# Two single-query attention blocks on one core: loads of 2 MB in place of 1 MB, scores by one product and one reduction, and a new order of the start

## The chip, the cores and the metric

The kernel runs on one core of a Trainium2 chip. The metric is the device time of one execution in microseconds. Of the kernel before there are six timed runs: median 1459.83 us, lowest 1456.88, highest 1462.38.

## What is computed

Two decoder blocks, A and B, each take one token x of 512 values and a cache of keys and values in bf16. Cut to what matters:

```
q      = x @ wq                                  # 32 heads of 128
scores = q . k_cache * 128 ** -0.5               # per head, over all cached rows
p      = softmax(scores)
o      = p @ v_cache
out    = o (all heads) @ wo                      # 512 values
A: 32 heads, each with its own cache of 32768 rows
B: 32 heads over 8 caches (4 heads share one), only the last 4096 rows of 32768
result = concatenate(A, B)
```

A's caches are 32 x 32768 rows x 256 bytes, twice: 537 MB. B reads 17 MB, and wq and wo of both blocks are 4 MB each. So each byte of a cache is read once and used for one (A) or four (B) multiplications.

## The kernel before, in words

A unit is one cache: 8 units of B (4096 rows, four queries) and 32 of A (32768 rows, one query), in that order. A unit is worked in chunks of 4096 rows: 1 for B, 8 for A, 264 chunks in all. A chunk of K or V is one DMA of 1 MB in which each of the 128 partitions takes 32 consecutive rows of the cache, 8 KB in one piece. All loads are issued by SP, in program order.

Step s of the main loop (L530) does k_phase for chunk s and v_phase for chunk s - 10 (V_LAG). So V is read ten chunks behind K, when the softmax of its unit is done. K chunks have 6 buffers (tiles kn), V chunks 5 (tiles vn).

The scores of an A chunk (k_phase, L401) are split by SPLITS over three engines, by tiles of 128 rows:

- 8 tiles on PE: transpose K (L380, tile ktp in PSUM), copy it to SBUF (L262, tile kts), multiply with the query (L384, tile qk).
- 17 tiles on VectorE, one instruction each: L450 multiplies a tile with qb, the query copied to all partitions, and sums it up, into Ssb. Its full product (junkd) is thrown away.
- 7 tiles: one VectorE product in f32 (L431, tile prod), and 7 sums on ScalarE (L440, junka).

A B chunk does all its 32 tiles on PE. After the last chunk of a unit come the maximum on VectorE (L300, mpart), a maximum over partitions on GpSimd (L274, mrow), a broadcast through PE (L266, bc), and the exponential on ScalarE (L283, P). For A this waits until the VectorE work of the next chunk is written out (LAG_MAX). VectorE's instructions are held in program order by dependencies that the function dve adds.

PV of A (v_phase, L498) multiplies four tiles at a time, 128x512, into PSUM (tile o); the last unit uses single tiles (L508, tile oT). finalize divides by the sum and multiplies with wo (L334), which is loaded in groups of eight heads, 1 MB in rows of 1 KB (L321).

The start (L521 to L526): three K chunks of B, then the whole query projection of B and of A. Each loads wq in four groups of 1 MB with rows of 2 KB (L194), and A's also builds qb, head by head, through a diagonal matrix on VectorE (L219) and a product on PE (L220).

A tile's buffer is handed on when the last instruction that reads it is done, and SP waits in order: a load that waits for its buffer holds back all loads behind it.

Of the kernel before, what the change touches and what calls it, by code (L numbers as in the profile page):

```python
# [17 lines left out]
CHUNK_ROWS = 4096  # L18
TG = 8
V_LAG = 10  # L20
K_BUFS = 6
V_BUFS = 5
KT_BUFS = 4
PROD_BUFS = 3
# [3 lines left out]
SPLITS = ((8, 17, 7),)  # L28
# [5 lines left out]
N_PRE = 3  # L34
FIN_DEFER = 1
CHAIN_DVE = 1
RECIP_DEFER = 4
TAIL_KPOOL = 1
WO_B_STEP = 6
QA_STEP = -1  # L40

# [29 lines left out]
def kernel(  # L71
# [54 lines left out]
    wpool = ctx.enter_context(tc.tile_pool(name="w", bufs=4))  # L126
# [23 lines left out]
    def make_model(name, x, wq, wo, hq, d_model, dout, out_off, want_qb):  # L150
# [17 lines left out]
        m.out_ps = None  # L168
        m.qb = cpool.tile([P, hq, DH], BF16, name=f"qb_{name}") if want_qb else None
# [3 lines left out]
    mA = make_model("A", A_x, A_wq, A_wo, HQA, D_A, DOUT_A, 0, use_vec)  # L173
    mB = make_model("B", B_x, B_wq, B_wo, HQB, D_B, DOUT_B, DOUT_A, False)

    def q_projection(m):
# [11 lines left out]
        xT_sb = cpool.tile([P, m.KC], BF16, name=f"xT_{m.name}")  # L188
        nc.vector.tensor_copy(xT_sb[:], xT_ps[:])
        Q_ps = ps_m.tile([P, m.HQ], F32, tag="misc", name=f"Q_ps_{m.name}")  # L190
        hpg = m.hpg
        for grp in range(m.n_groups):
            wq_sb = wpool.tile([P, m.KC, hpg * DH], BF16, tag="w", name=f"wq_{m.name}_{grp}")
            nc.sync.dma_start(  # L194
                out=wq_sb[:],
                in_=m.wq[:, grp * hpg * DH : (grp + 1) * hpg * DH].rearrange("(kc p) c -> p kc c", p=P),
            )
            for hl in range(hpg):
                h = grp * hpg + hl
                for kc in range(m.KC):  # L200
                    nc.tensor.matmul(
                        Q_ps[:, h : h + 1],
                        lhsT=wq_sb[:, kc, hl * DH : (hl + 1) * DH],
                        rhs=xT_sb[:, kc : kc + 1],
                        start=(kc == 0),
                        stop=(kc == m.KC - 1),
                    )
        nc.vector.tensor_copy(m.qT[:], Q_ps[:])
        if m.qb is not None:
            qT32 = cpool.tile([P, m.HQ], F32, name=f"qT32_{m.name}")  # L210
            nc.vector.tensor_copy(qT32[:], m.qT[:])
            HB = 4
            for h0 in range(0, m.HQ, HB):
                nh = min(HB, m.HQ - h0)
                qb_ps = ps_m.tile([P, HB, DH], F32, tag="misc", name=f"qb_ps_{m.name}_{h0}")
                for hl in range(nh):
                    h = h0 + hl
                    dg = junkpool.tile([P, P], BF16, tag="diag", name=f"diag_{m.name}_{h}")
                    nc.vector.tensor_scalar_mul(dg[:], ident[:], qT32[:, h : h + 1])  # L219
                    nc.tensor.matmul(qb_ps[:, hl, :], lhsT=ones_bf[:], rhs=dg[:], start=True, stop=True)  # L220
                nc.vector.tensor_copy(m.qb[:, h0 : h0 + nh, :], qb_ps[:, 0:nh, :])

    units = []
    for g in range(HKVB):
        units.append(
            _Unit(
                mB,
                len(units),
                B_k_cache[0, g, SKB - WIN : SKB, :],
                B_v_cache[0, g, SKB - WIN : SKB, :],  # L230
                REP,
                mB.qT[:, g * REP : (g + 1) * REP],
                mB.oT[:, g * REP : (g + 1) * REP],
                g * REP,
            )
        )
    for h in range(HA):
        units.append(
            _Unit(
                mA,  # L240
                len(units),
# [351 lines left out]
```

## Time and profile before

| | |
|---|---|
| median of six runs | 1459.83 us |
| the profiled execution | 1456.88 us |
| its span, first to last instruction | 1455.1 us |
| bytes read from HBM | 570.43 MB, 392 GB/s over the span |
| VectorE busy | 1242.7 us (85%) |
| PE busy | 1018.1 us (70%) |
| ScalarE busy | 878.2 us (60%) |
| median from issue to landing, K of A | 20.8 us |

How to read the views. The page gives for each engine the busy time, its share of the span and the count of instructions. A line of a DMA queue has packets, MB, and the time that the packets took as a share of 16 engines' time; q1 carries the program's loads, q8 and q14 carry instructions to the engines. A line of packets counts those under 512 B (mostly the completion signals of loads), under 2 KB and under 8 KB, each including the smaller ones. A line of windows has the stretch in us, its length, the busy time and the count of instructions of PE, PEld (weight loads), DVE (VectorE), ACT (ScalarE) and POOL (GpSimd), the granted PE clock, the DMA share and GB/s. A line of groups has source line, engine, operation, output and inputs, count, then busy time in us and mean ns of one, then the idle time before them and who ended it. A line of the order of time has start, duration, engine and line; SPq is SP's issue of a DMA.

### The profile page before, as it was taken

To read this page: it belongs to the slowest core of one execution; us is meant where nothing else is said; L and a number is where in the kernel's file an instruction comes from. 1 tells how busy PE (TensorE), PEld (TensorE's weight loads), DVE (VectorE), ACT (ScalarE), POOL (GpSimd) and SP (SyncE) were. 2 spreads that over 40 slices of the span, in tenths; PEclk is the share of its full clock that TensorE was granted. 3 is DMA by queue.
4 is the path that set the end of the run, shared out by engine and by line. 5 is a ranking of instruction groups with operands and counts; after the bars stand their busy time and mean duration, and the time that the engine had idled before them with its cause. 6 is when DMAs were issued, how large, how long until landed. Compare 5 with 4: busy or idle time off the path is not lost.

```text
span 1455.1 us, 31071 instructions
## 1 busy us (share of the span) xinstructions
PE 1018.1 (70%) x7872; PEld 506.1 (35%) x7872; DVE 1242.7 (85%) x9110; ACT 878.2 (60%) x4412; POOL 77.2 (5%) x128
## 2 busy tenths in 40 slices
PE   5684777677766677777676777767677676767775
PEld 5552333333333333333333333333333333333333
DVE  2588999989998998999999899999988899998982
ACT  1274777666566666576566565666666656666652
POOL 0113000000000000000000000000000000000000
PEclk7555988878788878798688786888877778888877
DMA  9699999999998999999998999999999899999995
GB/s 373 250 396 370 383 419 420 420 421 419 415 411 320 423 419 420 410 421 420 399 377 339 402 420 421 419 420 406 407 377 398 325 420 420 421 420 396 418 387 215
DMA packets 88762, 572.44 MB, mean 393 GB/s; under 512 B 8707, under 2 KB 16901, under 8 KB 20998
## 3 DMA queue, kind: packets, MB, share of 16 engines
q1 hardware_dynamic: 88582, 570.46, 95.9%
q8 instruction: 61, 1.00, 0.3%
q14 instruction: 119, 0.97, 0.2%
HBM read 570.43 MB, written 0.00 MB: 392 GB/s over the span
## 4 chain that ended last, share of the span: by engine, by line
issue 55%; DMA 20%; PE 14%; ACT 5%; POOL 4%; DVE 2%; SPq 1%; ACTq 0%; POOLq 0%; DVEq 0%
DMA kn<-in_A_k_cache_dram 10%; DMA vn<-in_A_v_cache_dram 9%; PE o L498 7%; ACT kts L262 3%; POOL mrow L274 3%; PE ktp L380 2%; ACT P L283 1%; DMA wq_B<-in_B_wq_dram 1%; PE bc_negb L266 1%; PE qk L384 1%; POOL srow L292 1%; PE oT L357 1%; DVE junkd L450 1%; PE S L384 0%; POOL nrow L276 0%
## 5 line engine op out<-in xcount | busy, mean ns | idle before, releaser
L450 DVE SCALAR_TENSOR_TENSOR junkd<-kn,qb_A 128x128 f32<-128x128 bf16 x4352 | 942.8, 284 | 0.0
L498 PE MATMUL o<-vn,P 128*4 128x512 bf16 x1984 | 605.6, 460 | 17.3 <-DMA vn<-in_A_v_cache_dram 17.1
L440 ACT ACTIVATE junka<-prod 128x128 bf16<-128x128 f32 x1792 | 527.4, 299 | 3.6 <-DVE prod L431 3.6
L262 ACT COPY kts<-ktp 128x1024 bf16<-128x1024 bf16 x266 | 268.8, 1010 | 328.4 <-PE ktp L380 310.6
L431 DVE TENSOR_TENSOR prod<-kn,qb_A 128x896 f32<-128x896 bf16 x256 | 278.7, 1089 | 131.8 <-DMA kn<-in_A_k_cache_dram 110.3
L450 DVE DVE_READ_ACCUMULATOR junkd<-kn,qb_A 128x1 f32 x4352 | 346.5, 80 | 0.0
L440 ACT ACTIVATION_READ_ACCUMULATOR junka<-prod 128x1 f32 x1792 | 340.3, 190 | 0.0
L384 PE MATMUL qk<-qT_A,kts 128*128 128x1 bf16 x2048 | 91.8, 166 | 284.0 <-ACT kts L262 283.6
L498 PEld LDWEIGHTS <-P 128*4 128x4 bf16 x1984 | 172.5, 95 | 301.4 <-issue 167.7
L380 PE MATMUL ktp<-ident,kn 128*128 128x128 bf16 x2304 | 212.8, 247 | 20.2 <-DMA kn<-in_A_k_cache_dram 14.0
L380 PEld LDWEIGHTS <-kn 128*128 128x128 bf16 x2304 | 157.1, 110 | 124.1 <-issue 77.8
L384 PEld LDWEIGHTS <-kts 128*128 128x128 bf16 x2304 | 79.9, 100 | 337.4 <-ACT kts L262 334.7
L274 POOL CROSS_LANE_REDUCE mrow<-mpart 128x1 f32<-128x1 f32 (+1 forms) x40 | 46.8, 1169 | 1260.8 <-DVE mpart L300 1256.2
L279 ACT COPY negb<-bc_negb 128x1 f32<-128x1 f32 (+1 forms) x40 | 6.4, 160 | 117.5 <-PE bc_negb L266 117.5
L357 PE MATMUL oT<-ident,o 4*128 4x1 f32 x248 | 43.1, 290 | 20.6 <-ACT o L354 20.6
L357 PEld LDWEIGHTS oT<-ident,o 4*128 4x128 f32 x248 | 40.4, 243 | 43.5 <-ACT o L354 43.5
L266 PE MATMUL bc_negb<-nrow,ones_row 1*128 1x1 f32 (+1 forms) x80 | 18.1, 294 | 48.0 <-POOL nrow L276 46.5
L367 ACT ACTIVATE oT_A<-oT,rinv 128x1 bf16<-128x1 f32 x32 | 8.4, 263 | 61.3 <-PE oT L357 45.8
L354 ACT COPY o<-o 4x512 f32<-4x512 f32 x31 | 17.8, 575 | 37.4 <-PE o L498 37.4
L266 PEld LDWEIGHTS bc_negb<-nrow,ones_row 1*128 1x128 f32 x80 | 14.8, 230 | 69.5 <-POOL nrow L276 66.2
L463 ACT COPY Ssb<-qk 128x8 f32<-128x8 f32 x256 | 37.3, 146 | 0.5 <-PE qk L384 0.5
L260 DVE COPY kts<-ktp 128x1024 bf16<-128x1024 bf16 x22 | 15.0, 687 | 22.1 <-PE ktp L380 19.2
(49 smaller groups left out, 252.8 us busy)
## 6 DMA issues: line engine op xcount, KB each, us to landing
kn<-in_A_k_cache_dram SPq DMA_DIRECT2D x256, 1024.0 KB, 20.8
vn<-in_A_v_cache_dram SPq DMA_DIRECT2D x256, 1024.0 KB, 20.6
kn<-in_B_k_cache_dram SPq DMA_DIRECT2D x8, 1024.0 KB, 12.9
vn<-in_B_v_cache_dram SPq DMA_DIRECT2D x8, 1024.0 KB, 11.2
wq_B<-in_B_wq_dram SPq DMA_DIRECT2D x4, 1024.0 KB, 13.8
wq_A<-in_A_wq_dram SPq DMA_DIRECT2D x4, 1024.0 KB, 10.4
wo_B<-in_B_wo_dram SPq DMA_DIRECT2D x4, 1024.0 KB, 16.5
wo_A<-in_A_wo_dram SPq DMA_DIRECT2D x4, 1024.0 KB, 21.7
```

Of the source, the lines that this page charges most:

```text
L262: nc.scalar.copy(dst, src)
L266: nc.tensor.matmul(bc_ps[:, 0:n], lhsT=ones_row[0:1, :], rhs=row[0:1, 0:n], start=True, stop=True)
L274: nc.gpsimd.tensor_reduce(out=mrow[:], in_=mpart[:], axis=AX.C, op=ALU.max)
L354: nc.scalar.copy(o4_sb[:], u.oT_ps[:, :])
L357: nc.tensor.matmul(src[:, 0:1], lhsT=o4_sb[0:PVG, jl * DH : (jl + 1) * DH], rhs=ident32[0:PVG, jl : jl + 1], start=(jl == 0), stop=(jl == ...
L380: nc.tensor.transpose(KTp[:, j8, :], KN[:, j0 + jj * tg + j8, :], ident[:])
L384: nc.tensor.matmul(dst_fn(jj * tg + j8), lhsT=KTs[:, j8, :], rhs=u.q_ap, start=True, stop=True)
L431: nc.vector.tensor_tensor(out=prod[:], in0=KN[:, jz : jz + nza, :], in1=qb.rearrange("p (o d) -> p o d", o=1).to_broadcast([P, nza, DH]), ...
L440: nc.scalar.activation(out=junk_a[:], in_=prod[:, jl, :], func=ACT.Copy, accum_out=S[:, t0 + jz + jl, :],)
L450: nc.vector.scalar_tensor_tensor(out=junk_d[:], in0=KN[:, j, :], scalar=1.0, in1=qb, op0=ALU.mult, op1=ALU.mult, accum_out=S[:, t0 + j, :],)
L463: nc.scalar.copy(S[:, t0 : t0 + npe, :], qk_ps[:, :, :])
L498: nc.tensor.matmul(u.oT_ps[:, :], lhsT=u.P_sb[:, t0 : t0 + PVG, :].rearrange("p t n -> p (t n)"), rhs=VN[:, jg * PVG : (jg + 1) * PVG, :]. ...
```

## The change

Sizes. A chunk of A has 8192 rows, so an A unit has 4 chunks, a DMA moves 2 MB, and each partition takes 16 KB in one piece. B's units stay one chunk of 4096 rows. K has 4 buffers and V 3, of 2 MB each. The split of an A chunk is 16, 34 and 14 tiles, twice that of before. V runs 5 chunks behind K.

Scores on VectorE. The 34 tiles are done by one product with bf16 output (L528, tile prodv, one buffer) and one reduction along the rows (L536). prod is bf16 as well (L510).

Order. After each of the first eight A units stands one B unit (INTERLEAVE). At the start the first group of A's query projection comes first, then two K chunks. The other seven groups of A and B are done one per step (q_group, L210 and L217). W buffers for wq and wo are 3 instead of 4. B's heads, which now finish between A's, are projected with wo in groups of eight into an SBUF tile (parts) and added up by VectorE; A keeps its sum in PSUM.

The diff, cut to its core:

```diff
-CHUNK_ROWS = 4096
+CHUNK_ROWS = 8192
-V_LAG = 10
-K_BUFS = 6
-V_BUFS = 5
+V_LAG = 5
+K_BUFS = 4
+V_BUFS = 3
-PROD_BUFS = 3
+PROD_BUFS = 2
+W_BUFS = 3
-SPLITS = ((8, 17, 7),)
+SPLITS = ((16, 34, 14),)
-N_PRE = 3
+N_PRE = 2
-RECIP_DEFER = 4
+RECIP_DEFER = 2
+INTERLEAVE = 1
+A_FIRST = 1
+Q_STAGED = 1
+Q_EARLY_STEPS = 1
...
-            prod = prodpool.tile([P, nza, DH], F32, tag="prod", name=f"prod_{u.idx}_{g}")
+            prod = prodpool.tile([P, nza, DH], BF16, tag="prod", name=f"prod_{u.idx}_{g}")
...
-        for jl in range(ndve):
-            j = npe + jl
-            junk_d = junkpool.tile([P, DH], F32, tag="junk_d", name=f"junkd_{u.idx}_{g}_{jl}")
+        if ndve:
+            pv = prodpool.tile([P, ndve, DH], BF16, tag="prodv", bufs=1, name=f"prodv_{u.idx}_{g}")
             dve(
-                nc.vector.scalar_tensor_tensor(
-                    out=junk_d[:],
-                    in0=KN[:, j, :],
-                    scalar=1.0,
-                    in1=qb,
-                    op0=ALU.mult,
-                    op1=ALU.mult,
-                    accum_out=S[:, t0 + j, :],
+                nc.vector.tensor_tensor(
+                    out=pv[:],
+                    in0=KN[:, npe : npe + ndve, :],
+                    in1=qb.rearrange("p (o d) -> p o d", o=1).to_broadcast([P, ndve, DH]),
+                    op=ALU.mult,
+                )
+            )
+            dve(
+                nc.vector.tensor_reduce(
+                    out=S[:, t0 + npe : t0 + npe + ndve, :].rearrange("p t n -> p (t n)"),
+                    in_=pv[:], axis=AX.X, op=ALU.add,
                 )
             )
...
+        q_setup(units[0].model)
+        q_setup(mB if units[0].model is mA else mA)
+        q_group(q_stage.pop(0)[0])
+        for s in range(min(N_PRE, n_steps, K_BUFS - 1)):
+            u0, g0 = chunks[s]
+            pre_kn[(u0.idx, g0)] = k_load(u0, g0)
...
+                if q_stage and s >= Q_EARLY_STEPS - 1:
+                    mm, _grp = q_stage.pop(0)
+                    q_group(mm)
```

More of the change, by code (lines that the diff above doesn't have):

```diff
@@ new lines @@
+    units = []
+    if INTERLEAVE:
+        gb = 0
+        for h in range(HA):
+            units.append(make_a_unit(h, len(units)))
+            if gb < HKVB:
+                units.append(make_b_unit(gb, len(units)))
+                gb += 1
+        while gb < HKVB:
+            units.append(make_b_unit(gb, len(units)))
+            gb += 1
+    else:
+        for g in range(HKVB):
+            units.append(make_b_unit(g, len(units)))
+        for h in range(HA):
+            units.append(make_a_unit(h, len(units)))
@@ L405, in k_phase @@
             KN = k_load(u, g)
-        vec_ok = N == 1 and u.model.qb is not None and J % TG == 0
+        split = SPLITS[a_chunk_cnt[0] % len(SPLITS)]
+        vec_ok = (
+            N == 1
+            and u.model.qb is not None
+            and sum(split) == J
+            and split[0] % u.tg == 0
+        )
         if not vec_ok:
```

214 lines of the change are left out of this document (140 added, 74 removed).

## The prediction

> **What bounds the kernel now.** I read the page's totals first, then the DMA queues, then short windows of the start, the end and one slow place in the middle, then the groups of VectorE. The totals name two busy resources, the DMA engines and VectorE:
>
> ```profile
> span 1455.1 us, 31071 instructions
> PE 1018.1 (70%) x7872; PEld 506.1 (35%) x7872; DVE 1242.7 (85%) x9110; ACT 878.2 (60%) x4412; POOL 77.2 (5%) x128
> q1 hardware_dynamic: 88582, 570.46, 95.9%
> q8 instruction: 61, 1.00, 0.3%
> ```
>
> The loads keep 16 DMA engines 95.9% busy. VectorE has 1243 us of work in 1455, less than the transfers take. In the undisturbed middle the engines are full, at about 420 GB/s:
>
> ```profile
> 500.00:525.00 25.00, 20.31 (x94) 8.95 (x94) 22.12 (x165) 12.19 (x63) 0.99 (x3) 0.52 1.01 419
> ```
>
> So a load that only comes earlier gains nothing there. The end shows more. The DMA view of the last 12 us, one window of them (PE, PEld, VectorE, ScalarE and GpSimd busy, clock, DMA share, GB/s), and the order of time behind it:
>
> ```profile
> DMA packets 52, 0.38 MB, mean 31 GB/s; under 512 B 7, under 2 KB 7, under 8 KB 7
> q1 hardware_dynamic: 51, 0.36, 7.2%
> q8 instruction: 1, 0.02, 0.5%
> 1440.00:1442.00 2.00, 1.01 (x32) 0.93 (x32) 0.00 (x0) 0.00 (x0) 0.00 (x0) 0.50 0.06 25
> 1450.30 1.01 PE L508 MATMUL oT<-P,vn 128*128 128x1 bf16 x32 [1.46 <-DMA vn<-in_A_v_cache_dram]
> 1452.95 0.26 SPq L562 DMA_DIRECT2D out_dram<-res_sb  x1
> ```
>
> From 1437.5 to 1449.5 the loads fill 7.2% of 16 engines, which is one engine (1/16 is 6.25%). It carries 44 rows of 8 KB alone while 15 engines have finished, and the last V chunk waits for it. The one instruction fetch of these 12 us is there too: 0.5% of 16 x 12 us is 0.96 us. In the middle the same engine shows itself after the reload of wo (1 KB rows), where SP sits in one issue for 12 us and the traffic falls to a sixteenth:
>
> ```profile
> 450.37 12.35 SPq L392 DMA_DIRECT2D kn<-in_A_k_cache_dram  x1
> 458.00:460.00 2.00, 0.56 (x5) 0.55 (x6) 2.00 (x12) 0.11 (x1) 1.30 (x2) 0.91 0.06 25
> ```
>
> I read this as one engine that lags 8 to 13 us behind the others, because every load gives each engine the same sixteenth and this one fetches PE's code as well (in the last 12 us only PE has instructions left). If so, the kernel's time is that engine's work. I sum it, with durations from two windows, one with 8 KB rows only (475 to 700 us) and one with the 2 KB rows of wq (12 to 31 us), and the window in which the traffic sets in:
>
> ```profile
> DMA packets 12902, 94.07 MB, mean 418 GB/s; under 512 B 1429, under 2 KB 1429, under 8 KB 1429
> q1 hardware_dynamic: 12874, 93.76, 100.8%
> DMA packets 3677, 7.33 MB, mean 386 GB/s; under 512 B 113, under 2 KB 114, under 8 KB 3675
> q1 hardware_dynamic: 3675, 7.29, 103.8%
> 2.00:4.00 2.00, 0.00 (x0) 0.00 (x0) 0.00 (x0) 0.02 (x1) 0.00 (x0) 1.00 0.74 295
> ```
>
> An 8 KB row takes 0.314 us (44 rows in 7.2% of 192 us; 0.317 in the middle window, 3629 us over 11,445 rows). A 2 KB row takes 315.6 us / 3562 = 0.0886 us. For a 1 KB row I take 0.055, between half of that and the whole. One engine then has 528 K and V loads x 8 rows x 0.314 = 1326 us, 8 wq loads x 32 rows x 0.0886 = 23, 8 wo loads x 64 x 0.055 = 28, and 61 fetches x 0.96 = 59: 1436 us. Its time goes from about 2 us to 1450, 1448 us. The difference of 12 is idle time, and I find most of it at the start:
>
> ```profile
> 50.00:52.00 2.00, 0.92 (x5) 0.41 (x4) 1.24 (x4) 0.00 (x0) 0.00 (x0) 0.50 0.10 41
> 54.00:56.00 2.00, 0.96 (x32) 0.87 (x31) 1.01 (x3) 1.18 (x8) 1.22 (x3) 0.50 0.00 0
> 58.00:60.00 2.00, 1.86 (x29) 1.33 (x27) 0.69 (x1) 1.10 (x3) 0.68 (x1) 0.50 0.00 0
> 64.00:66.00 2.00, 2.00 (x34) 2.00 (x32) 0.95 (x2) 0.68 (x5) 0.68 (x1) 0.50 0.30 41
> ```
>
> Nothing moves from 51 to 60 us, and little around 64: the B units come first, their K loads fill the six buffers, and SP waits for PE and the softmaxes.
>
> **The change part by part.**
>
> **Rows of 16 KB.** 256 K and 256 V loads of A become 128 and 128, with half the rows, each 16 KB. Bytes are the same. What can go is the fixed part of a row. From 2 KB to 8 KB a row grows by 0.314 - 0.0886 = 0.225 us for 6 KB, so 8 KB more cost 0.300 and a 16 KB row 0.614, against 0.628 for two of 8 KB. The bounds are 0.601 (no fixed part at all) and 0.628 (a row goes out as two packets of 8 KB). I take 0.614, on the line of the two measured sizes. One engine carries 16,384 x 2 / 16 = 2048 such rows: 2048 x 0.0135 = **28 us less** (0 to 55).
>
> **PE's fetches.** PE's order has 15,041 rows before and after. The 61 fetches stay, **0 us**. VectorE's order falls from 4760 rows to 542, but its fetches are not seen in the tail on the late engine.
>
> **The start.** The order of SP's loads before, where the idle time lies (kn are K chunks, vn V chunks), and after from the first row:
>
> ```order
> L321 DMA wo_B_1221<-in_B_wo_dram 128x8x512
> L392 DMA kn_0_1229<-in_B_k_cache_dram 128x4096
> L392 DMA kn_0_1332<-in_A_k_cache_dram 128x4096
> L392 DMA kn_1_1412<-in_A_k_cache_dram 128x4096
> L392 DMA kn_2_1491<-in_A_k_cache_dram 128x4096
> L486 DMA vn_0_1564<-in_B_v_cache_dram 128x4096
> ```
>
> ```order
> L466 DMA kn_0_213<-in_A_k_cache_dram 128x8192
> L466 DMA kn_1_215<-in_A_k_cache_dram 128x8192
> L210 DMA wq_B_217<-in_B_wq_dram 128x4x1024
> L210 DMA wq_B_327<-in_B_wq_dram 128x4x1024
> L210 DMA wq_B_436<-in_B_wq_dram 128x4x1024
> L466 DMA kn_2_472<-in_A_k_cache_dram 128x8192
> L210 DMA wq_B_547<-in_B_wq_dram 128x4x1024
> L466 DMA kn_3_583<-in_A_k_cache_dram 128x8192
> L210 DMA wq_A_658<-in_A_wq_dram 128x4x1024
> L466 DMA kn_0_723<-in_B_k_cache_dram 128x4096
> ```
>
> Before, the first V stood behind eight B chunks and three A chunks; now one wq group is followed by 2 MB chunks with wq loads between them. I followed this by hand at 420 GB/s. The first chunk lands near 12 us, VectorE takes 8.3 us each (below), K buffers come free at 20, 29, 38 and 46 us, while the loads issued by then last until 45, 50, 60 and 65. So nothing starves, with one narrow place: PE waits for A's first softmax, behind it in PE's order stands the use of wq_A's third group, and SP's wo_B load waits for that buffer. That softmax holds a slow step:
>
> ```profile
> 124.90 13.94 POOL L274 CROSS_LANE_REDUCE mrow<-mpart 128x1 f32<-128x1 f32 x1 [37.34 <-DVE mpart L300]
> ```
>
> If it takes 14 us again, PE is free at 63 to 64 us, just when the queue runs dry. I keep 4 of the 12 idle us: **8 us less** (0 to 12).
>
> **VectorE.** One chunk before and after (junkd is a 128-element product with its sum, prod and prodv are products of several tiles, Ssb the scores):
>
> ```order
> L450 SCALAR_TENSOR_TENSOR junkd_4_15_2698,Ssb_2204<-kn_4_2630,qb_A 128x128
> L450 SCALAR_TENSOR_TENSOR junkd_4_16_2700,Ssb_2204<-kn_4_2630,qb_A 128x128
> L310 RECIPROCAL rrow_2713<-srow_2288 1x1
> L431 TENSOR_TENSOR prod_5_2741<-kn_5_2719,qb_A 128x896
> L450 SCALAR_TENSOR_TENSOR junkd_5_0_2757,Ssb_2204<-kn_5_2719,qb_A 128x128
> ```
>
> ```order
> L536 TENSOR_REDUCE Ssb_1514<-prodv_0_1584 128x34
> L510 TENSOR_TENSOR prod_1_1652<-kn_1_1611,qb_A 128x1792
> L528 TENSOR_TENSOR prodv_1_1682<-kn_1_1611,qb_A 128x4352
> L536 TENSOR_REDUCE Ssb_1514<-prodv_1_1682 128x34
> L345 RECIPROCAL rrow_1704<-srow_1447 1x1
> ```
>
> The 34 small products of 8192 rows become one product of 4352 elements and one reduction. Their prices from these groups:
>
> ```profile
> L431 DVE TENSOR_TENSOR prod<-kn,qb_A 128x896 f32<-128x896 bf16 x256 | 278.7, 1089 | 131.8 <-DMA kn<-in_A_k_cache_dram 110.3 <-ACT junka L440 10.6 <-ACT Ssb L463 8.5
> L260 DVE COPY kts<-ktp 128x1024 bf16<-128x1024 bf16 x22 | 15.0, 687 | 22.1 <-PE ktp L380 19.2 <-ACT kts L262 2.6
> L300 DVE TENSOR_REDUCE mpart<-Ssb 128x1 f32<-128x256 f32 x32 | 13.2, 412 | 1.4 <-ACT Ssb L463 1.2
> L221 DVE CAST qb_A<-qb_ps_A 128x512 bf16<-128x512 f32 x8 | 5.5, 686 | 0.4 <-PE qb_ps_A L220 0.4
> ```
>
> From 256 to 896 elements the price grows by (1089 - 412) / 640 = 1.058 ns each. The reduction of 4352 is 1.089 + 3456 x 0.001058 = 4.75 us. The products now write bf16, and with 16-bit data on every side a copy of 1024 elements costs what one of 512 costs with f32 in it (687 against 686 ns). So I take the products at half rate: 1.09 us for 1792 elements and, as for 2176, 2.44 for 4352. A chunk is 8.3 us, or 2.04 + 4.75 + 4.75 = 11.5 if they stay at full price. The one engine needs (1455 - 28 - 8) / 128 = 11.1 us per chunk of K and V. So VectorE is hidden, **0 us**, and stays hidden until a chunk passes about 10.7 (other VectorE work, 49 us over 128 chunks, takes 0.4). [...]
>
> **Fewer buffers.** The PV products of before:
>
> ```profile
> L498 PE MATMUL o<-vn,P 128*4 128x512 bf16 x1984 | 605.6, 460 | 17.3 <-DMA vn<-in_A_v_cache_dram 17.1
> ```
>
> 4 K and 3 V buffers of 2 MB hold 14 MB, against 11 MB before. A K buffer comes back 8.3 us after landing and is wanted again four chunks on, 44 us later. V's PV needs about 16 matmuls x 460 ns = 7 us of 33. Hidden; cost 0.
>
> **The tail.** The last V chunk has 64 matmuls instead of 32 behind its landing, 1.01 us more: **+1**.
>
> Sum: 1455.1 - 28 - 8 + 1 = 1420 us span. The profiled execution took 1456.88 us, 1.8 more than its span, and the median of the runs is 1459.83, 3.0 above that execution. So 1420 + 1.8 + 3.0 = **1425 us**. A measurement here can tell about 0.2%, 3 us, from no change.
>
> **The rivals.**
>
> *Rows go out as 8 KB packets.* Then 28 us stay: 1453. For it: no row of this trace carries K or V in a larger packet. Against: 8 KB rows stayed whole, and nothing shows a limit there. It is the upper end.
>
> *No single engine is the bound.* Then the mean engine counts: its 95.9 + 0.3% of 1455.1 is 1400 us, less 28, with 2 ahead, 5 behind and 4 idle: 1383 + 4.8, so 1388. The tail row of one engine alone speaks against it. [...]
>
> *VectorE becomes the bound* (slower). If the broadcast operand qb keeps the products at full price, a chunk is 11.5 us, above the 10.7 where it decides: 12 to the first chunk + 128 x 11.5 + 49 + 17 for the last softmax, 256 matmuls and the end = 1550, with 4.8, 1555. For it: no TENSOR_TENSOR of the trace runs at half rate, since all write f32. Against: the two copies above.
>
> *The narrow place at the start, or a softmax that comes late at unit boundaries.* PE would hold K buffers; some 15 us come back: 1440.
>
> **How the numbers follow.** Forecast 0.62; 8 KB packets 0.18; start or boundaries 0.08; no single engine 0.06; VectorE 0.06. The range goes from 1408 (a 16 KB row of about 0.606, halfway to its lower bound) to 1454 (the 8 KB case); it leaves out the rivals at 1388 and 1555 and the far ends of the row price, about 0.17. Within 3 us of 1460 falls only the edge of the 8 KB case, 0.03. Faster 0.91, slower 0.06.
>
> **What would show it.** Right: about 34,800 packets of K and V (128 x 256 + 128 x 16) instead of 528 x 128 = 67,584, steady windows near 428 GB/s, no empty windows before 70 us, q8 still at 61 packets, one engine alone at the end, TENSOR_TENSOR of 4352 near 2.4 us, VectorE near 1110 us. Wrong: packets of 8 KB still, q8's engine not last, VectorE above 95%, or K loads that wait for VectorE in the middle.

## The result, and the profile after

The changed kernel takes 1373.85 us (median of 8 runs, 1373.45 to 1374.2) against 1459.42 us of the kernel before in the same jobs (16 runs). The ratio is 0.9412, 95% interval [0.9403, 0.9421]. The forecast was 1425 us with a range from 1408 to 1454: the direction was right, the size was not. 86 us went, 35 were forecast.

The page of the changed kernel, totals and DMA queues:

```profile
span 1372.3 us, 21605 instructions
PE 976.9 (71%) x7872; PEld 501.3 (37%) x7872; DVE 1079.6 (79%) x541; ACT 869.6 (63%) x4293; POOL 101.5 (7%) x128
DMA packets 51824, 571.82 MB, mean 417 GB/s; under 512 B 4611, under 2 KB 12805, under 8 KB 16902
q1 hardware_dynamic: 51718, 570.45, 98.7%
q8 instruction: 61, 1.00, 0.3%
q14 instruction: 45, 0.37, 0.1%
```

The engines are fuller (98.7% against 95.9%), and 51,824 - 16,902 = 34,922 packets have 8 KB or more: the rows of 16 KB went out whole (128 x 256 of them, 128 x 16 rows of 8 KB and the 61 + 45 packets of q8 and q14 make the same 34,922). TensorE's fetches (q8, which rises to 94 where number 3 adds instructions of TensorE) stayed at 61. The row that the prediction did not use is the last one. Before, it read:

```profile
q14 instruction: 119, 0.97, 0.2%
```

q14 brings instructions in pieces of 8 KB (0.97 MB in 119 packets). 74 of 119 pieces are gone, and VectorE's instructions fell from 9,110 to 541. The prediction named VectorE's order in rows and left it at that.

Windows of the changed kernel at its start and at its end (length, busy time and count of PE, PEld, VectorE, ScalarE and GpSimd, clock, DMA share, GB/s):

```profile
0.00:25.00 25.00, 10.17 (x176) 8.32 (x176) 16.79 (x24) 12.93 (x60) 1.09 (x8) 1.00 0.93 363
50.00:75.00 25.00, 16.87 (x171) 10.49 (x171) 19.11 (x38) 10.78 (x47) 2.37 (x6) 0.95 1.03 404
1347.00:1352.00 5.00, 4.40 (x21) 1.61 (x19) 0.15 (x1) 1.32 (x4) 0.55 (x2) 1.00 1.00 426
1352.00:1357.00 5.00, 3.56 (x80) 3.15 (x81) 0.00 (x0) 0.44 (x3) 0.00 (x0) 0.88 0.51 213
1357.00:1362.00 5.00, 2.01 (x74) 1.93 (x73) 0.00 (x0) 0.00 (x0) 0.00 (x0) 0.50 0.06 26
1362.00:1367.00 5.00, 1.99 (x75) 1.91 (x73) 0.00 (x0) 0.00 (x0) 0.00 (x0) 0.50 0.06 23
```

The empty stretch at 50 to 75 us is gone (189 GB/s there before, row in number 8). The end still shows one DMA engine working alone (0.06 is one sixteenth), now for about 10 us. So the form of the bound stayed, one engine alone at the end, and that end comes 86 us earlier.

VectorE's groups after (busy us, mean ns of one, idle time before them):

```profile
L536 DVE TENSOR_REDUCE Ssb<-prodv 128x34 f32<-128x4352 bf16 x128 | 599.8, 4686 | 4.3
L528 DVE TENSOR_TENSOR prodv<-kn,qb_A 128x4352 bf16<-128x4352 bf16 x128 | 309.4, 2418 | 0.0
L510 DVE TENSOR_TENSOR prod<-kn,qb_A 128x1792 bf16<-128x1792 bf16 x128 | 139.7, 1091 | 206.8 <-DMA kn<-in_A_k_cache_dram 170.3 <-ACT junka L519 29.2 <-ACT kts L297 3.3
```

4.69, 2.42 and 1.09 us, within 2% of what was worked out beforehand. VectorE waits for K 170 us in all. The other way round it is less: SP's K loads (line 466) wait for VectorE 23 times, 89 us in all, and the DMA share of 98.7% says that the transfers hardly notice.

Now the two places where the prediction had found the late engine alone, closer: windows of 3 us of the kernel before, in 40 slices of 75 ns. A slice shows GB/s where a packet starts (109 for 8 KB, 218 for 16 KB). The first is in the middle, behind the reload of wo:

```profile
GB/s 0 109 0 0 0 109 0 0 0 0 109 0 0 0 109 0 0 0 109 218 0 0 0 0 0 0 0 0 0 0 0 109 0 0 0 109 0 0 0 109
q1 hardware_dynamic: 8, 0.06, 6.0%
q8 instruction: 1, 0.02, 2.2%
q14 instruction: 1, 0.01, 0.7%
```

The second is in the tail:

```profile
GB/s 0 0 0 109 0 0 0 0 109 0 0 0 109 0 218 0 109 0 0 0 109 0 0 0 109 0 0 0 109 0 0 0 109 0 0 0 0 109 0 0
q1 hardware_dynamic: 10, 0.07, 5.9%
q8 instruction: 1, 0.02, 2.0%
```

The lone engine starts a row every four to five slices, 0.31 us. In the tail the 16 KB fetch of q8 falls between two beats and the beat goes on: the fetch is on another engine. In the middle, the piece of q14 (the packets put it at the fourth 109) takes a beat for itself, and the row behind it takes 13 slices, 0.97 us, in place of four. In the trace's packets the piece takes 0.33 us and the row 0.66 us more than its neighbours, 0.99 us together. That is where 1 us per fetch could come from, on the engine that ends last. A fetch of q8 (the 218) runs beside this row, so this window alone does not say which of the two fetches slowed it; the tail, where the rows beside the q8 fetch keep their 0.31 us, speaks for q14.

### The profile page after: what moved, and what is told of

The parts are those of the page before. It is cut to its first block, busy times and chain, and to the rows that moved or that the text cites. A ratio compares the mean times of both kernels' runs of the same rounds, so it can differ in the third digit from the quotient of the medians.

```text
span 1372.3 us, 21605 instructions
## 1 busy us (share of the span) xinstructions
PE 976.9 (71%) x7872; PEld 501.3 (37%) x7872; DVE 1079.6 (79%) x541; ACT 869.6 (63%) x4293; POOL 101.5 (7%) x128
## 2 busy tenths in 40 slices
DMA packets 51824, 571.82 MB, mean 417 GB/s; under 512 B 4611, under 2 KB 12805, under 8 KB 16902
## 3 DMA queue, kind: packets, MB, share of 16 engines
q1 hardware_dynamic: 51718, 570.45, 98.7%
## 4 chain that ended last, share of the span: by engine, by line
issue 78%; POOL 6%; PE 5%; DMA 4%; ACT 3%; DVE 3%; SPq 0%; ACTq 0%; POOLq 0%; DVEq 0%
POOL srow L327 5%; PE o L579 2%; DMA kn<-in_A_k_cache_dram 2%; DMA vn<-in_A_v_cache_dram 2%; PE bc_negb L301 2%; ACT P L318 2%; POOL mrow L309 1%; DVE Ssb L536 1%; ACT kts L297 1%; POOL nrow L311 1%; DVE prodv L528 1%; PE ktp L454 0%; ACT negb L314 0%; ACT junka L519 0%; DVE prod L510 0%
## 5 line engine op out<-in xcount | busy, mean ns | idle before, releaser
L536 DVE TENSOR_REDUCE Ssb<-prodv 128x34 f32<-128x4352 bf16 x128 | 599.8, 4686 | 4.3
L519 ACT ACTIVATE junka<-prod 128x128 bf16<-128x128 bf16 x1792 | 525.7, 302 | 10.9 <-DVE prod L510 10.9
L519 ACT ACTIVATION_READ_ACCUMULATOR junka<-prod 128x1 f32 x1792 | 347.7, 194 | 0.0
L579 PEld LDWEIGHTS <-P 128*4 128x4 bf16 x1984 | 187.6, 98 | 409.3 <-issue 274.2
L528 DVE TENSOR_TENSOR prodv<-kn,qb_A 128x4352 bf16<-128x4352 bf16 x128 | 309.4, 2418 | 0.0
L510 DVE TENSOR_TENSOR prod<-kn,qb_A 128x1792 bf16<-128x1792 bf16 x128 | 139.7, 1091 | 206.8 <-DMA kn<-in_A_k_cache_dram 170.3
L454 PE MATMUL ktp<-ident,kn 128*128 128x128 bf16 x2304 | 167.5, 229 | 18.2 <-DMA kn<-in_A_k_cache_dram 17.7
L454 PEld LDWEIGHTS <-kn 128*128 128x128 bf16 x2304 | 140.4, 103 | 52.7 <-DMA kn<-in_A_k_cache_dram 26.1
L309 POOL CROSS_LANE_REDUCE mrow<-mpart 128x1 f32<-128x1 f32 (+1 forms) x40 | 19.8, 495 | 1186.8 <-DVE mpart L335 1186.8
L327 POOL CROSS_LANE_REDUCE srow<-rowsum 128x1 f32<-128x1 f32 (+1 forms) x40 | 72.4, 1810 | 56.8 <-ACT P L318 56.8
```

Source lines behind the costliest of these rows:

```text
L309: nc.gpsimd.tensor_reduce(out=mrow[:], in_=mpart[:], axis=AX.C, op=ALU.max)
L327: nc.gpsimd.tensor_reduce(out=srow[:], in_=rowsum[:], axis=AX.C, op=ALU.add)
L454: nc.tensor.transpose(KTp[:, j8, :], KN[:, j0 + jj * tg + j8, :], ident[:])
L510: nc.vector.tensor_tensor(out=prod[:], in0=KN[:, jz : jz + nza, :], in1=qb.rearrange("p (o d) -> p o d", o=1).to_broadcast([P, nza, DH]), ...
L519: nc.scalar.activation(out=junk_a[:], in_=prod[:, jl, :], func=ACT.Copy, accum_out=S[:, t0 + jz + jl, :],)
L528: nc.vector.tensor_tensor(out=pv[:], in0=KN[:, npe : npe + ndve, :], in1=qb.rearrange("p (o d) -> p o d", o=1).to_broadcast([P, ndve, DH]) ...
```

## The experiments

Four theories stood at first. **A**: the engine that carries VectorE's instructions set the end before. **B**: the order of the start and the stalls. **C**: the forecast's, TensorE's fetches set the end. VectorE's own time was to be kept apart from all of them. The edits are shown cut to their core. Later A split into **S** (each engine's instructions come through a DMA engine of their own, and only the latest counts) and **T** (one DMA engine carries them all).

### 1. Tiles one by one again, all else as changed

```diff
-            dve(nc.vector.tensor_tensor(out=pv[:], ...))
-            dve(nc.vector.tensor_reduce(out=S[...], in_=pv[:], ...))
+            for jl in range(ndve):
+                dve(nc.vector.scalar_tensor_tensor(out=junk_d[:], ..., accum_out=S[:, t0 + npe + jl, :]))
```

> The changed kernel with one thing undone: VectorE's 34 tiles of a chunk go one by one again (34 SCALAR_TENSOR_TENSOR with an f32 result, each with its accumulator read, some 8,700 instructions in the run) in place of one product and one TENSOR_REDUCE. By the rows, VectorE's time for a chunk hardly moves: 909 us for 4,352 tiles before (1,242.7 busy less 278.7 of products and some 55 of the rest), so 209 ns a tile and 7.1 us for 34, against 2.42 + 4.69 = 7.1 us now; rows, order and queues stay. Theory A (the DMA engine that carries VectorE's instructions set the end of the kernel before; the fetches of VectorE's queue, q14, fall from 119 to 45 with the change): q14 rises again to about 115 packets and the time by 35 to 60 us, to 1,410 to 1,430. Theory B (the gain over the forecast came from the order of the start and from the stalls that went): within 8 us of the changed kernel, 1,374 to 1,382. Theory C (the forecast's: the engine that carries TensorE's instructions ends last, in both kernels): 1,374, since q8 stays at 61 packets.

Measured 1418.69 us, 44.8 more than the changed kernel. Its totals and queue:

```profile
PE 994.8 (70%) x7872; PEld 505.1 (36%) x7872; DVE 1106.2 (78%) x8989; ACT 869.7 (61%) x4293; POOL 57.2 (4%) x128
q14 instruction: 111, 0.91, 0.2%
1397.00:1402.00 5.00, 3.92 (x94) 3.51 (x94) 0.00 (x0) 0.53 (x3) 0.00 (x0) 0.95 0.11 46
1402.00:1407.00 5.00, 1.98 (x75) 1.90 (x72) 0.00 (x0) 0.00 (x0) 0.00 (x0) 0.50 0.06 26
```

VectorE is nearly as busy as in the changed kernel (1106 against 1080 us, 78% against 79% of the span), so its time is not the cause; the count of its instructions is what changed. The time is in A's range and outside those of B and C, which fall as the main cause.

### 2. Product and reduction alone, on the kernel before

```diff
+            prod = prodpool.tile([P, nza, DH], BF16, ...)
+            dve(nc.vector.tensor_tensor(out=pv[:], ...))        # 17 tiles in one
+            dve(nc.vector.tensor_reduce(out=S[...], in_=pv[:], ...))
-            for jl in range(ndve): ... scalar_tensor_tensor(...)
```

> The kernel before with one part of the change alone: VectorE's 17 tiles of a chunk as one product and one TENSOR_REDUCE, with bf16 products; 8 KB rows, old depths and old order stay. Theory A (VectorE's fetches made one DMA engine late): q14 falls to about 50 packets and the time to 1,405 to 1,420, most of the gain without the long rows or the new order. Theory B (order and stalls): the stalls at the start and at the reloads stay, 1,450 to 1,460. Theory C (TensorE's fetches set the end): 1,450 to 1,460, the few us of steady VectorE waits at most.

Measured 1407.61 us against 1460.06: 52.5 us, with 8 KB rows, the old order and the empty start still there. Its queue:

```profile
q14 instruction: 55, 0.45, 0.1%
50.00:75.00 25.00, 19.98 (x264) 17.30 (x264) 9.34 (x20) 11.69 (x59) 6.18 (x13) 1.00 0.45 179
```

### 3. More TensorE instructions

The kernel as changed, with 33 dummy products a chunk into a spare PSUM column.

```diff
+            for _ in range(33):
+                nc.tensor.matmul(qk_ps[:, npe, :], lhsT=ident[:], rhs=ones_bf[:, 0:1], start=True, stop=True)
```

> The changed kernel with 33 dummy matmuls of one column added to each of the 128 chunks, into a spare column of the same PSUM tile: 8,448 more TensorE instructions, so about 33 more fetches of 16 KB on q8 (61 now); TensorE has the room (71% busy). Theory C (the DMA engine that carries TensorE's instructions ends last; the forecast priced its 61 fetches at 59 us, 0.97 us each): q8 rises to 94 and the time by about 32 us, to 1,406. Theory A (TensorE's fetches don't delay the engine that ends last): within 5 us of the changed kernel, 1,370 to 1,379. Theory B: the same as A.

Measured 1381.68 us, 7.8 more where C said 32.

```profile
q8 instruction: 94, 1.54, 0.5%
PE 1091.3 (79%) x12096; PEld 616.3 (45%) x12096; DVE 1078.1 (78%) x541; ACT 868.6 (63%) x4293; POOL 69.4 (5%) x128
```

0.24 us per fetch, above A's 5 us, so A's range was missed too; but C, the forecast's reading, falls. The packets say below that the 7.8 us are waiting, not fetching; TensorE's 115 us of added work may cause it.

### 4 and 5. GpSimd instructions

```diff
+        for gi in range(66):
+            nc.gpsimd.memset(gp_row[0:1, gi : gi + 1], float(gi))
+        nc.gpsimd.tensor_tensor(out=gp_sum[:], in0=gp_sum[:], in1=gp_row[:], op=ALU.add)
```

> The changed kernel with dummy work for GpSimd added to each of the 128 chunks: 66 memsets of one element each and one sum over them, some 8,600 instructions that nothing waits for, as many as VectorE's tiles had. Nothing else changes. Theory A in its general form (any engine's instructions that come in 8 KB fetches make the DMA engine that carries them late): q14 rises by about 67 packets, to 112, and the time by 20 to 65 us, to 1,394 to 1,440, with TensorE, VectorE and ScalarE as busy as before. Theories B and C: within 4 us of the changed kernel, 1,370 to 1,378; if GpSimd's own chain at a unit's end came late by the dummy work, waits on mrow and srow would show it.

Measured 1664.05 us, and it tells nothing of the fetches. The dummy work depended on nothing and came to stand ahead of the first softmax's maximum in GpSimd's order, so that TensorE and SP stood still behind that softmax: the narrow place of the prediction, at full size. A window of this run:

```profile
300.00:350.00 50.00, 0.58 (x2) 0.50 (x2) 0.00 (x0) 0.15 (x1) 47.19 (x1211) 1.00 0.00 1
```

The second form ties it to the chunk, with a copy of the chunk's scores ahead of half of the memsets:

```diff
+        nc.gpsimd.tensor_copy(gp_row[0:1, 0:ndve], S[0:1, t0 + npe : t0 + npe + ndve, :]...)
```

> The dummy GpSimd work again (66 memsets of one element and one sum a chunk, on top of the changed kernel), now tied to its chunk by a copy of 34 of that chunk's scores ahead of half of them, so that it can't all run at the start. By the row of the run before (89 ns a memset) it takes GpSimd some 7 us of each chunk's 10.7, and the two reductions of a unit's softmax may wait that long behind it. Theory A (any engine's 8 KB fetches make the DMA engine that carries them late): q14 at 112 or more, and the time up by 20 to 65 us, 1,394 to 1,440, with the end set by one late DMA engine. Theory B or C: within 8 us of the changed kernel, up to 1,382.

Measured 1397.18 us, 23.3 more than the changed kernel.

```profile
PE 962.4 (69%) x7872; PEld 496.0 (36%) x7872; DVE 1080.3 (77%) x541; ACT 869.0 (62%) x4293; POOL 426.3 (31%) x8833
q14 instruction: 113, 0.92, 0.2%
1380.00:1385.00 5.00, 1.98 (x74) 1.90 (x72) 0.00 (x0) 0.00 (x0) 0.00 (x0) 0.50 0.06 26
1385.00:1390.00 5.00, 1.98 (x74) 1.89 (x72) 0.00 (x0) 0.00 (x0) 0.00 (x0) 0.50 0.06 23
```

One DMA engine ends alone again. Work that computes nothing of use, on an engine that is 31% busy, costs 23 us, in A's range. Not all of it need be the fetches: TensorE's waits for the maximum of the softmax (tile nrow) rose as well, from 97 to 156 us in all. The model below needs no such part.

### 6 and 7. Fewer ScalarE instructions

```diff
-SPLITS = ((16, 34, 14),)
+SPLITS = ((16, 40, 8),)      # and ((16, 44, 4),)
```

> The changed kernel with six more of each chunk's 64 tiles on VectorE and six fewer on ScalarE (16, 40 and 8 in place of 16, 34 and 14): ScalarE loses 12 instructions a chunk, 1,536 in the run, about 12 fetches of q14 (45 to 33). VectorE's chunk rises by the rows from 8.2 us to (40 of 34) x 7.1 + 0.6 = 9.0 us of 10.7. Theory A (what is left of the late engine is ScalarE's fetches): 6 to 14 us faster than the changed kernel, 1,360 to 1,368. Theory B or C, or a bound by VectorE: 1,372 to 1,385.

> The same with ten tiles moved (16, 44 and 4): 2,560 instructions of ScalarE fewer, about 20 fetches fewer (45 to 25); VectorE's chunk 9.5 us of 10.7. Theory A: 12 to 22 us faster than the changed kernel, 1,352 to 1,362, unless VectorE's waits (its share of the span goes to 90%) give some back. Theory B or C: 1,372 or more, since VectorE and what waits for it only get later.

Measured 1365.64 and 1362.31 us, 8.2 and 11.5 less than the changed kernel; the second is a little short of its range. The first run's queue and tail, then the second's:

```profile
q14 instruction: 33, 0.27, 0.0%
1348.00:1353.00 5.00, 1.99 (x72) 1.90 (x72) 0.00 (x0) 0.00 (x0) 0.00 (x0) 0.50 0.51 213
1353.00:1358.00 5.00, 1.99 (x75) 1.91 (x73) 0.00 (x0) 0.00 (x0) 0.00 (x0) 0.50 0.06 23
```

```profile
PE 979.4 (72%) x7872; PEld 510.6 (38%) x7872; DVE 1246.9 (92%) x541; ACT 501.9 (37%) x1733; POOL 118.1 (9%) x128
q14 instruction: 25, 0.20, 0.0%
1345.00:1350.00 5.00, 2.01 (x71) 1.93 (x72) 0.00 (x0) 0.00 (x0) 0.00 (x0) 0.50 0.67 279
1350.00:1355.00 5.00, 1.98 (x75) 1.90 (x72) 0.00 (x0) 0.00 (x0) 0.00 (x0) 0.50 0.37 154
```

The lone engine shrinks to some 4 us and then is gone: in the second, several engines still work in the last 5 us. In the first, the share of 0.51 ahead of that is half of the engines. Making VectorE busier (92% of the span) made the kernel faster, which no theory of VectorE's time gives.

### 8. The order alone, on the kernel before

The diff's lines on INTERLEAVE, A_FIRST, Q_STAGED and the partial sums, with 8 KB rows, old depths, old products.

> The kernel before with the change's order alone (queries in groups, units of the two models by turns, late sums), at 8 KB rows, old depths, and VectorE's tiles one by one. Theory A (VectorE's fetches set the end): the start and the reloads gain their 8 to 12 us at most and q14 stays at 119, 1,446 to 1,456. Theory B (order and stalls are most of the gain): 1,415 to 1,435. Theory C: as the forecast's start term, 1,450.

Measured 1439.35 us against 1459.98: 20.6 us less, between what A and B said, so both missed. Its start:

```profile
50.00:75.00 25.00, 14.45 (x135) 9.68 (x132) 22.77 (x156) 15.44 (x76) 3.26 (x6) 1.00 1.02 412
100.00:200.00 100.00, 75.84 (x685) 40.52 (x683) 83.18 (x601) 65.24 (x316) 6.51 (x14) 0.85 1.01 412
```

The same windows of the kernel before:

```profile
50.00:75.00 25.00, 19.40 (x283) 16.56 (x283) 9.44 (x20) 12.76 (x60) 6.87 (x14) 0.64 0.49 189
100.00:200.00 100.00, 61.98 (x569) 32.03 (x570) 90.71 (x685) 62.32 (x325) 16.89 (x6) 0.70 0.96 387
```

At 420 GB/s that is 13 us of traffic in the first window ((412 - 189) x 25 / 420) and 6 in the second.

### 9. The rows alone

The kernel as changed, with the old chunk size, depths and split.

```diff
-CHUNK_ROWS = 8192
+CHUNK_ROWS = 4096
...                          # depths and W_BUFS as before
-SPLITS = ((16, 34, 14),)
+SPLITS = ((8, 17, 7),)
```

> The changed kernel with 8 KB rows, the old depths and the old split again; product, reduction and order stay. The forecast's row term (2,048 rows of 16 KB per engine at 0.0135 us less than two of 8 KB) says 28 us: 1,402. Theory A, with the parts measured so far: the kernel before less 52 for the product and reduction and less 21 for the order gives 1,387, so the rows are worth 13 us, if the parts add up; q14 stays near 55. Theory B has no price for the rows; 1,387 fits it only if the order gains more where VectorE's instructions are few.

Measured 1393.22 us, so the long rows, with the depths that go with them, bring 19.4 us, between 28 and 13. Slices of this run, then of the changed kernel:

```profile
GB/s 365 405 421 420 414 420 419 415 421 411 421 420 414 422 420 421 421 421 420 420 421 366 422 421 421 421 421 420 421 422 419 359 421 420 421 421 420 421 421 243
```

```profile
GB/s 376 401 428 426 420 426 425 420 426 419 426 428 410 427 428 428 426 428 427 426 428 394 428 427 427 427 427 429 426 428 427 382 427 426 427 428 428 428 421 212
```

421 against 427 to 428 in the full slices.

### 10. Half of the tiles one by one

```diff
+        if a_chunk_cnt[0] % 2 == 0:   # tiles one by one
+        else:                         # product and reduction
```

> The changed kernel with every second chunk's 34 tiles one by one again, half of the first experiment: q14 rises by about 33, to 78. Theory A in two forms. If VectorE's and ScalarE's instructions come through the same DMA engine, the price goes by the count, 33 x 0.68 = 22 us: 1,396. If each has its own DMA engine and only the latest counts, VectorE's 37 fetches barely pass ScalarE's 34 and the time rises by 0 to 6 us: 1,374 to 1,380.

Measured 1386.39 us, 12.5 more than the changed kernel: between both forms, so both missed.

```profile
q14 instruction: 78, 0.64, 0.1%
```

So 33 fetches cost 12.5 us and the next 33 cost 32.3.

### 11. No sums on ScalarE

```diff
-SPLITS = ((16, 34, 14),)
+SPLITS = ((16, 48, 0),)
+            dve(nc.vector.tensor_tensor(out=ph[:], in0=pv[:, :, 0 : DH // 2], in1=pv[:, :, DH // 2 : DH], op=ALU.add))
-                    in_=pv[:], axis=AX.X, op=ALU.add,
+                    in_=ph[:], axis=AX.X, op=ALU.add,
```

> The changed kernel with ScalarE's sums gone: 48 of a chunk's 64 tiles go to VectorE as one product, one addition of the upper half of each row to the lower (bf16, rounded once more), and a reduction of half the elements. ScalarE loses 3,584 instructions, 28 fetches (q14 45 to 17). VectorE by the rows: 48 of 34 of 2.42 = 3.4, an addition of 3,072 elements at the product's price 1.7, a reduction of 3,072 at 3.3: 8.4 us a chunk, as now. Theory A: with 0.57 to 0.68 us a fetch 16 to 19 us faster than the changed kernel, 1,355 to 1,358, and down to 1,350 if the waits on VectorE that the run with 44 tiles had go too; two engines end together at the end. Theory B or C: 1,372 to 1,376.

Measured 1362.16 us, no faster than with 4 sums a chunk on ScalarE, so a miss.

```profile
PE 966.4 (71%) x7872; PEld 500.3 (37%) x7872; DVE 1126.4 (83%) x541; ACT 362.1 (27%) x709; POOL 115.4 (8%) x128
q14 instruction: 17, 0.14, 0.0%
1345.00:1350.00 5.00, 2.67 (x100) 2.59 (x98) 0.00 (x0) 0.00 (x0) 0.00 (x0) 0.50 0.53 223
```

Fetches fell by 8 more and nothing moved: no engine ends alone any more. But they don't end together either: a share of 0.53 in the window is about half of the 16 engines, and these set the end now. Whose fetches they carry is said below. It also gives the size of a piece: 3,584 ScalarE instructions less are 28 pieces less, 128 instructions each.

### 12 and 13. Is it the buffers?

> A control for the next run: the first experiment (tiles one by one on top of the changed kernel, 1,418.7) with two buffers for wq and wo in place of three. Both forms of theory A: within 8 us of it, 1,415 to 1,427.

> The same with a fourth V buffer of 2 MB in the place of the third W buffer. Half of the tiles cost 12.5 us and all of them 44.8, so the second 33 fetches cost more than twice the first. Theory A1 (while the late engine's lag fits into what the V buffers hold ahead, its fetches cost 0.3 to 0.4 us each; above that the next loads are issued too late, and all engines stop, the late one too): with one more buffer the lag may grow further, and the time falls to 1,393 to 1,408. Theory A2 (a fetch of VectorE's instructions simply costs the late engine 0.7 to 1 us, whatever the buffers): as the control, 1,415 to 1,427.

```diff
-W_BUFS = 3
+W_BUFS = 2
-V_BUFS = 3
+V_BUFS = 4                   # the second of the two only
```

Both are number 1 with other buffers. Measured 1451.61 and 1450.53 us. The control missed its range by 25 us, since wo's loads now wait for a buffer and hold SP (first row, the control). Between the two, the fourth V buffer brings 1.1 us, within the spread of the control's own runs (1450.1 to 1452.6), though SP then waits for PV about half as long (292 against 563 us in all) and for K's buffers instead (second row, with four):

```profile
SPq L362 <- PE qk L458: 87.4, 3, 30.1
```

```profile
SPq L466 <- DVE junkd L529: 656.2, 105, 12.9
```

That speaks against a limit of the V buffers (A1), but weakly: with two W buffers SP stands for some 30 us at a time, and a late engine could catch up there, an estimate of mine that no run shows.

### 14 to 16. One DMA engine for all, or one for each

Number 14 is number 11 with GpSimd's dummy work, 15 is number 10 with it, and 16 is number 1 with ScalarE's 14 sums moved to VectorE in the manner of number 11.

```diff
+            dve(nc.vector.tensor_tensor(out=pz[:], in0=prod[:, :, 0 : DH // 2], in1=prod[:, :, DH // 2 : DH], op=ALU.add))
+            dve(nc.vector.tensor_reduce(out=S[:, t0 + jz : t0 + jz + nza, :]..., in_=pz[:], axis=AX.X, op=ALU.add))
-            for jl in range(nza): ... nc.scalar.activation(...)
```

> GpSimd's dummy work (66 memsets of one element and a sum a chunk, tied to its chunk) on top of the kernel that has no ScalarE sums (1,362.2), with some 69 fetches for GpSimd and 6 for ScalarE where the run with the dummy work and ScalarE's sums (1,397.2) had 69 and 34. Theory S (each engine's instructions come through a DMA engine of their own, and only the latest of these counts): GpSimd's is the latest in both, so 1,397 again, 1,392 to 1,400. Theory T (one DMA engine carries all of the fetches, and the price goes by their sum): 28 fetches fewer at about 0.6 us, 1,377 to 1,386.

> The same dummy work on top of the kernel with every second chunk's tiles one by one (1,386.4): VectorE has 37 fetches, ScalarE 34, GpSimd 69. Theory S: GpSimd's DMA engine passes VectorE's, 1,394 to 1,402. Theory T: 68 fetches more than 1,386.4, at the 0.34 us that they cost alone or more, 1,408 to 1,430.

> The changed kernel with all 34 tiles of a chunk one by one (1,418.7) and without ScalarE's sums: its 14 tiles are added up by VectorE, upper half of each row to the lower and a reduction of what is left. VectorE 73 fetches, ScalarE 6 in place of 34; VectorE's chunk 2.6 + 7.1 = 9.7 us. Theory S: VectorE's DMA engine sets the end as before, 1,416 to 1,425. Theory T: 28 fetches fewer, 1,396 to 1,406.

Measured 1396.72, 1396.56 and 1420.36 us: S in all three. The queue of number 14, then 15, then 16:

```profile
q14 instruction: 86, 0.70, 0.1%
```

```profile
q14 instruction: 146, 1.19, 0.2%
```

```profile
q14 instruction: 85, 0.70, 0.1%
```

86 and 146 fetches give the same time, and GpSimd's 69 are the same in both; 85 and 86 give 24 us of difference, and in one they are mostly VectorE's and in the other GpSimd's.

### What the runs give together

With 128 instructions to a fetch, and at 16 KB rows: VectorE's price is (1418.7 - 1386.4) / 33 = 0.98 us a fetch (numbers 1 and 10), ScalarE's is 8.2 / 12 = 0.68 (number 6). Taken back to no fetch at all, 1386.4 - 37 x 0.98 = 1350 and 1373.85 - 34 x 0.68 = 1351, the same base from both. GpSimd's from it: (1397.2 - 1350.5) / 69 = 0.68. With 20 us for 8 KB rows and 20 for the old order, the model is: base, plus the largest product of fetches and price. A count of fetches is an engine's count of instructions over 128.

| | largest | model | measured |
|---|---|---|---|
| before | VectorE 71 | 1350.5 + 20 + 20 + 70 = 1460 | 1459.4 |
| order alone (8) | VectorE 71 | 1350.5 + 20 + 70 = 1440 | 1439.4 |
| product and reduction alone (2) | ScalarE 34 | 1350.5 + 20 + 20 + 23 = 1414 | 1407.6 |
| 8 KB rows (9) | ScalarE 35 | 1350.5 + 20 + 24 = 1394 | 1393.2 |
| no ScalarE sums, tiles one by one (16) | VectorE 73 | 1350.5 + 72 = 1422 | 1420.4 |
| dummy work, half of the tiles (15) | GpSimd 69 | 1350.5 + 47 = 1397 | 1396.6 |
| 4 sums on ScalarE (7) | ScalarE 14 | 1350.5 + 9 = 1360 | 1362.3 |
| no ScalarE sums (11) | ScalarE 6 | 1350.5 + 4 = 1355 | 1362.2 |

The base, the prices and the two terms of 20 (19.4 in number 9, 20.6 in number 8) come from runs of this list, so not every line is a test. Tests are numbers 8, 15 and 16, within 2 us each. Number 2 is 6 us off: with few VectorE instructions the order is worth 14, not 20. The last row shows where the model, as far as it counts q14 alone, ends: below some 1362 us no engine is late alone, and another limit holds.

The packets of the traces say where these prices come from. Look at the K or V row that starts within 25 ns of the end of a piece of q14, after 80 us. It takes longer than the middle row of its size, by about 0.66 us behind one kind of piece and by about 0.38 us behind another:

| | rows 0.55 to 0.80 us longer | VectorE's fetches | rows 0.30 to 0.50 us longer | ScalarE's and GpSimd's fetches |
|---|---|---|---|---|
| before | 68 | 71 | 39 | 34 + 1 |
| half of the tiles (10) | 36 | 37 | 35 | 34 + 1 |
| no ScalarE sums (11) | 4 | 4 | 11 | 6 + 1 |
| no ScalarE sums, tiles one by one (16) | 66 | 73 | 8 | 6 + 1 |
| dummy work (5) | 6 | 4 | 88 | 34 + 69 |

The counts go together without being equal: before, 10 of the 117 pieces after 80 us have neither kind of row behind them, two of these (at 151.7 us) no row at all. With the piece itself, 0.31 to 0.33 us, that is 0.98 us for VectorE and 0.69 for ScalarE, and 0.66 in number 5, where most are GpSimd's: the prices that the times gave. A fetch of TensorE takes 1.07 us in the median, before and after, and the row behind it is 0.49 us longer, so one costs 1.56 us.

The packets also tell the DMA engines apart. On a busy engine a packet starts 3 to 15 ns before the one ahead of it ends (3 to 4 ns on the lone engine in the tail of the kernel before, 12 behind the piece at 460 us), and each load of K or V gives each engine eight rows and a completion signal (in that tail a signal follows every eight rows). So each engine's packets can be followed from the end back to 110 us. This is a reconstruction from times and no view, and it can confuse two engines for a stretch (in the kernel before it does so too often to be used), but three traces come out plainly:

- Number 16: the engine that ends last (1412.7 us) carries 68 of the 80 pieces of q14 and none of TensorE's fetches, and is never idle. No other engine has more than two pieces, and each of them is idle for 29 to 39 us.
- The changed kernel: the engine that ends last (1366.1 us) carries 27 of 42 pieces, each with the shorter delay of ScalarE's kind, and none of TensorE's fetches, and is idle for 0.2 us.
- Number 11: eight engines end at 1351.5 to 1354.3 us and carry 44 of TensorE's 56 fetches of that stretch; the other eight end at 1343.5 to 1347.3. TensorE's fetches are thus spread over about eight engines, and 61 / 8 x 1.56 = 12 us on the base gives 1362.4, where numbers 7 and 11 stopped.

In number 3 the same sum is 94 / 8 x 1.56 = 18 us, less than ScalarE's 23, so its fetches should cost nothing. There the engine that ends last is idle for 7.6 us, in place of 0.2, which is about the 7.8 us.

## Why the prediction was wrong, point by point

- **The step that failed** is the one under "PE's fetches": that the late engine "fetches PE's code as well", so that its 61 fetches stay and count 0 us, while VectorE's "fetches are not seen in the tail on the late engine". The late engine was VectorE's, and TensorE's fetches, by number 11's packets, are spread over about eight engines, 12 us on each, not 59 on one. VectorE's engine carried 71 fetches at 0.98 us, 70 us; after the change it carries 4, and ScalarE's engine is the latest with 34 at 0.68, 23 us. That is 47 us of the 86, and numbers 1 and 2 measure the step by itself: 44.8 and 52.5 us. The forecast had 0.
- **Why it looked right.** The tail has one fetch, and it is TensorE's, since VectorE has nothing left to run there. A fetch that can't occur in a window is not shown to be elsewhere by its absence. The sum of the late engine's work closed (1436 + 12) by luck, because errors met: 59 us of fetches in place of 70, and 0.314 us for an 8 KB row in place of 0.311 to 0.312, which is the middle one in the trace's packets, over 4,224 rows 8 to 13 us. The 1 KB rows took 0.047 us and not 0.055, 4 us more.
- **What a fetch cost**: 0.98 us for VectorE (numbers 1 and 10), 0.68 for ScalarE (number 6) and GpSimd (number 5), as long as their DMA engine is the latest. For TensorE no cost of a fetch shows in the time of the changed kernel, whose latest engine carries none of its fetches, and some 12 us, by the sum above, do in numbers 7 and 11, where the engines with its fetches end last.
- **Rows of 16 KB**: mechanism right (whole packets, 427 to 428 GB/s in full slices), size off: 28 forecast, 19.4 measured. The packets give 2,048 x (2 x 0.311 to 0.312 - 0.613) = 18 to 23 us; the 0.314 came from a rounded share of a tail window that also holds small packets.
- **The start**: 8 forecast, 14.4 (1407.6 of number 2 to 1393.2 of number 9, which differ by the order) to 20.6 measured (number 8). The windows of number 8 put 13 us in the empty stretch, and 6 more behind it, at 100 to 200 us, where I had counted nothing. The narrow place with 14 us in mrow did not come (the longest mrow of the changed kernel takes 1.39 us).
- **VectorE**: prices right to 2%, hidden as forecast; the rival with 11.5 us a chunk did not hold, since the products ran at half price (2.42 us for 4352 elements, against 4.75 by the prices of before).
- **Fewer buffers, the tail**: as forecast, no cost seen in the changed kernel. Number 12 shows how near W is to it: with tiles one by one, one W buffer less costs 33 us.
- **Sum by parts measured**: 52.5 for product and reduction (number 2), 14.4 for the order on top of it (number 9), 19.4 for the rows: 86.3 us, against 85.6. The three are steps of one way from the kernel before to the changed one, so they have to close but for the difference between the medians of the kernel before.

Still open: why the row behind a fetch takes longer, and why by 0.66 us behind VectorE's and 0.38 us behind ScalarE's and GpSimd's. It was counted, not explained. That each of these engines has a DMA engine of its own rests on the times of numbers 14 to 16 and on the packets followed as above; no view names the engine of a packet. What the last engine waits for in number 3 stays open.

## What to carry to other kernels

In a kernel that keeps all 16 DMA engines busy with equal shares, count the instructions of every engine, not only their time: here each 128 of VectorE, ScalarE or GpSimd were a fetch that cost one DMA engine 0.7 to 1 us, and the latest of these DMA engines set the end. If a tail shows one DMA engine alone, compare q8 and q14 and ask whose instructions they are, in a window where that engine runs. Merging small VectorE instructions was worth more here than their busy time says (44.8 us in number 1, where VectorE was busy for only 27 us more), and fewer fetches paid down to the point at which no DMA engine ended alone; the split of 16, 44 and 4 tiles gave 1362.3 us, 11.5 less than the change itself.

## What the runs showed of the hardware

- Instructions of VectorE, ScalarE and GpSimd come on q14 in pieces of 8 KB (before, 0.97 MB in 119 packets), 128 of them to a piece by the counts: 66 pieces for 8,448 of VectorE's (number 1), 28 for 3,584 of ScalarE's (number 11), 68 for 8,705 of GpSimd's (number 5). TensorE's come on q8 in 16 KB (before, 1.00 MB in 61 packets; 33 more for number 3's dummy products).
- A fetch cost its DMA engine 0.98 us for VectorE (numbers 1 and 10) and 0.68 for ScalarE (number 6) and GpSimd (number 5), while the fetch itself takes 0.31 to 0.33 us in the packets; the rest is the row behind it, 0.66 or 0.38 us longer.
- Fetches of different engines did not add up: with 69 of GpSimd's, 28 fewer of ScalarE's (number 14 against 5) or 33 more of VectorE's (number 15) moved the time by less than 1 us.
- TensorE's fetch of 16 KB takes 0.96 us in the tail of the kernel before and 1.07 us in the median, and does not disturb the beat of the late engine (the tail window above, where its rows keep their 0.31 us). In number 11 these fetches lie on about eight of the 16 DMA engines (44 of 56 on the eight that end last).
